# A fused attention and two-MLP kernel: weight conversion in two places of a slot, earlier stores and splits, identity products in front, the last output block in halves

## The chip, the cores and the metric

The kernel runs on one core of a Trainium2 chip. The metric is the device time in microseconds (us) of one execution. A core has TensorE (PE, matrix products into PSUM), VectorE (DVE), ScalarE (ACT), GpSimd (POOL) and SyncE (SP); DMAs are issued by SP, ACT and POOL queues. Each engine carries out its own instructions in the order in which the program issues them, and waits for semaphores of the others.

## The reference, cut to what matters

```python
B, H, S, Ns, D = 8, 8, 512, 32, 64
a = softmax(scale * x @ state.T);   xread = a @ state      # 512 rows per batch and head
a2 = softmax(scale * state @ x.T);  sread = a2 @ x         # 32 "states' rows" per batch and head
t = concat([xread, sread])          # 8 batches x 544 rows, 512 wide
t = ((t @ w1) * (t @ w2)) @ w3 @ w_out                      # first MLP
h = t @ w_in                                               # second MLP, 2048 wide
out = (h * clip(h + 3, 0, 6) / 6) @ w_out2
```

All inputs and the output are float32.

## The kernel before, in words

Products in full precision are made from a high part (`fp32r`, rounded) and a low part (the rest): three products high x high, high x low, low x high (`mm3`). ACT makes the high part (`rnd`, L71), DVE the low part (`rest`, L79). The program has four stages.

**Front, 0 to about 115 us.** Weights of the first MLP come in as 64-bit words (layout of the host), and DVE and ACT convert them to float32 (`Pipe`, L142 to L155), unit by unit. w3 @ w_out is multiplied out once (`ps_w`, L419), and attention of batch 0 and 1 runs between the units.

**Blocks, about 115 to 480 us.** One block `b` is one batch of 512 rows; it has eight slots `m` (block 0 starts at slot 4). Below, (b,m) is slot m of block b. One slot is, in TensorE's order: 12 products for `ps_ab` (two banks); the first half of the `x2` products of a slot issued two slots earlier (6); in even slots the 32 small products `ps_p` of a later slot pair; in some slots attention products of the next batch (`ps_s` in slot 0, `ps_e` in slot 4, `ps_r` in slot 6); the second half of the `x2` products. DVE and ACT serve it: `asb` (ACT copy of one bank), `ab` (DVE product of both banks, L529), `abh`/`abl` (high and low part), `ph`/`pl` (the same of `ps_p`), and the steps of attention. PSUM banks of the tag `b` go round in a ring of four: in slot (b,1) `ps_ab` takes the banks of `ps_p` of slot (b,0), which `pl` (DVE) frees; in slot 4, `ps_e` takes those of `ps_ab`, which `ab` frees.

Beside it runs `stream2`, which converts the 16 units of the second MLP's weights and stores them to DRAM for later. It is a generator, cut into pieces by `yield n`, where n is a cost. `before()` in a slot, after `ab`, adds `ROOM[m]` to an allowance and takes pieces until it is used up. One unit is on DVE: `ts` and `hd` (L473, L475), `w` (L478), the sum into `w` (L489, or L491 and L493), `cm` (four quarter sums, L507 to L510), and two low parts `sl` (768 and 1024 columns); on ACT: `sh` (two high parts, called by `parts`), and `hd` (unpack of the next unit, L445); on SP: one load of 1 MB, and the stores of `sh` and `sl` (`out_of_parts`).

**States, 480 to about 540 us.** `s_block` runs the 256 states' rows through the first MLP. It needs their high and low part `xs_hl`, which are made at the top of the last block (L749, L750).

**Second MLP, to the end.** Pairs of blocks go through a seven-product scheme (Strassen's, Winograd's form) with the stored weights: `gates` (L936), then `output` (L1097), for four pairs. The last pair also carries the states' rows. At the very end DVE adds and transposes the last two result tiles (`both(21, q)`), and SP stores them by four DMAs.

Of the kernel before, what the change touches and what calls it, by code (L numbers as in the profile page):

```python
# [19 lines left out]
def attn_moe_kernel(tc, xt_d, xn_d, bd_d, wa, wb, wc, wi, wo, out):  # L20
# [56 lines left out]
    def rest(out_, in_, hi, eng):  # L77
        e = nc.gpsimd if eng == "P" else nc.vector
        e.tensor_tensor(out=out_, in0=in_, in1=hi.bitcast(F32), op=ALU.subtract)  # L79
# [39 lines left out]

    ORDER = "oaoaoaoawwppppwwpppp"  # L120

    ROOM = (10, 7, 6, 6, 2, 6, 11, 9)


    class Pipe:
# [45 lines left out]


    x_t, A_t, st_t = {}, {}, {}
    xs_r = None
    room = 0

    def load_x(b):
# [6 lines left out]
    def attention(b, fine=False):  # L184
# [49 lines left out]
        def sread_out(ps):  # L234
            if b == B - 1:
                nc.scalar.copy(out=xs_r[:, :, b * NS:], in_=ps[:, :4 * NS].rearrange("p (c n) -> p c n", c=4))
                return
            xs = att.tile([128, 4, NS], F32, tag="xs", name="xs")
            nc.scalar.copy(out=xs.rearrange("p c n -> p (c n)"), in_=ps[:, :4 * NS])
            nc.sync.dma_start(out=xsd[:, :, b * NS:(b + 1) * NS], in_=xs)  # L240
# [103 lines left out]

    with tc.manual_schedule():
        make_identity(nc, ident)


        main = open_pool("main", bufs=1, side=left, reuse_waits="tile")
# [81 lines left out]
        def stream2():  # L431

            units = [x for u in range(8) for x in ((wi, u), (wo, u))]
            raws, hds = {}, {}

            def load(i):
                if i < len(units):
                    raw = raws[i] = cvs.tile([128, 4160], U16, tag="raw", name="raw", bufs=2)[:, :4100]
                    nc.sync.dma_start(out=raw[:, 1:4097], in_=units[i][0][units[i][1]].bitcast(U16))

            def unpack(i):
                if i < len(units):
                    hd = hds[i] = cvs.tile([128, 1024], U16, tag="hd", name="hd", bufs=2)
                    top = raws[i].bitcast(BF16)[:, 4:].rearrange("p (n k) -> p n k", k=4)[:, :, 0]
                    nc.scalar.activation(out=hd.bitcast(BF16), in_=top, func=AF.Prelu, scale=2.0 ** -112,  # L445
                                         alpha=2.0 ** 32)

            load(0)
            load(1)
            yield 0  # L450
            unpack(0)
            yield 0
            v = nc.vector
            def parts(h, w, cm):
                rnd(h[:, :768], w[:, :768], "A")
                rnd(h[:, 768:], cm, "A")

            def out_of_parts(src, u, h, l):
                for hl, t in enumerate((h, l)):
                    to = swi[u][hl].rearrange("p s k f -> p s (k f)") if src is wi else swo[hl][:, :, u, :]  # L460
                    for at, of, n in ((0, 2, 5), (5, 0, 2)):
                        nc.sync.dma_start(out=to[:, at:at + n, :],
                                          in_=t.bitcast(F32)[:, 256 * of:256 * (of + n)].rearrange("p (s e) -> p s e", e=256))

            prev = None
            for i in range(len(units) + 1):
                more = i < len(units)
                if more:
                    src, u = units[i]
                    hd, raw = hds.pop(i), raws[i]  # L470
                    ts = cvs.tile([128, 1024], U16, tag="ts", name="ts")
                    w = cvs.tile([128, 1024], F32, tag="w", name="w", bufs=2)
                    v.tensor_scalar(out=ts, in0=hd, scalar1=3, scalar2=0xFF80, op0=ALU.logical_shift_left,  # L473
                                    op1=ALU.bitwise_and)
                    v.tensor_scalar(out=hd, in0=hd, scalar1=3, scalar2=None, op0=ALU.logical_shift_left)  # L475
                    yield 2
                    g = raw.bitcast(U32).rearrange("p (n k) -> p n k", k=2)[:, :1024, 1]
                    v.scalar_tensor_tensor(out=w, in0=g, scalar=2.0 ** -36, in1=ts.bitcast(BF16), op0=ALU.mult,  # L478
                                           op1=ALU.mult)
                    raws.pop(i)  # L480
                    load(i + 2)
                if prev:
                    h, l = (cvs.tile([128, 1792], F32R, tag=f"s{hl}", name=f"s{hl}") for hl in "hl")
                    parts(h, *prev[2:])
                yield 3
                if more:
                    hb = hd.bitcast(BF16)
                    if src is wi:
                        v.tensor_tensor(out=w, in0=w, in1=hb, op=ALU.add)  # L489
                    else:  # L490
                        v.scalar_tensor_tensor(out=w[:, :512], in0=w[:, :512], scalar=-1.0, in1=hb[:, :512],  # L491
                                               op0=ALU.mult, op1=ALU.subtract)
                        v.tensor_tensor(out=w[:, 512:], in0=w[:, 512:], in1=hb[:, 512:], op=ALU.add)  # L493
                    unpack(i + 1)
                    yield 3
                if prev:
                    rest(l[:, :768], prev[2][:, :768], h[:, :768], "V")
                    yield 2
                    rest(l[:, 768:], prev[3], h[:, 768:], "V")
                    out_of_parts(*prev[:2], h, l)  # L500
                    yield 3
                if not more:
                    return
                cm = cvs.tile([128, 1024], F32, tag="cm", name="cm")
                a12, a22, a11, a21 = (w[:, 256 * k:256 * k + 256] for k in range(4))
                s1, s2, s4, s3 = (cm[:, 256 * k:256 * k + 256] for k in range(4))
                v.tensor_tensor(out=s1, in0=a21, in1=a22, op=ALU.add if src is wi else ALU.subtract)  # L507
                v.tensor_tensor(out=s3, in0=a11, in1=a21, op=ALU.subtract)
                v.tensor_tensor(out=s2, in0=s1, in1=a11, op=ALU.subtract)
                v.tensor_tensor(out=s4, in0=a12, in1=s2, op=ALU.subtract if src is wi else ALU.add)  # L510
                prev = src, u, w, cm
                yield 4
# [225 lines left out]
        for b in range(B):  # L738
# [5 lines left out]
                close_pool("cvs")  # L744
                wsq = open_pool("wsq", bufs=1, side=right, reuse_waits="tile")
            if b == B - 1:
                t = att.tile([128, T, DM], F32R, tag="xn", name="xs_hl").rearrange("p (i a) f -> p i (a f)", i=2)
                xs_h, xs_l = (t[:, i].rearrange("p (k f) -> p k f", k=KD) for i in range(2))
                rnd(xs_h, xs_r, "A")  # L749
                rest(xs_l, xs_r, xs_h, "V")  # L750
                s_block()
                close_pool("wsq")
                close_pool("att")
                xb = open_pool("xb", bufs=1, side=right, reuse_waits="tile")
                first = combos(0)
            A = A_t.pop(b)
            for m in range(0 if b else 4, M1):
                if m == (6 if b else 7) and b + 2 < B:
                    load_x(b + 2)

                def before():
                    nonlocal room
                    step()
                    room += ROOM[m]
                    while room > 0:
                        room -= next(second, 99)

                vn = 4 * b + m // 2 + 1

                def mid_():  # L770
                    if vn < 4 * B and m % 2 == 0:
                        p_mm(vn)
                        p_split(vn)
                    step()
                slot(b, m, A, before, mid_)
                if b == 0:
                    step()
# [239 lines left out]
        def output(p, ring, side):  # L1017
# [34 lines left out]
            def both(k, q):  # L1052
                result(k, q)
                leave(k, q)
# [28 lines left out]
            for v in range(28):  # L1083
# [4 lines left out]
                name = ("d1", "d3", "d2", "d3", "d2", "d1", "d2")[i]  # L1088
                hl = two(ring[v % 3])

                def main():
                    for q in range(2):
                        for k in range(2):
                            n = 2 * u + k
                            wh, wl = (t[:, 128 * q:128 * q + 128] for t in w_at(base, 8 * i + n))
                            for z, (a, x) in enumerate(((wh, hl[0]), (wh, hl[1]), (wl, hl[0]))):
                                nc.tensor.matmul(d[name][q], a, x[:, k, :], start=i < 3 and n == 0 and z == 0,  # L1097
                                                 stop=n == NG - 1 and z == 2, skip_group_check=True)

                def more():  # L1100
# [11 lines left out]
                                                 stop=i > 1 and n == NG - 1 and z == 2, skip_group_check=True)  # L1112
                if i == 6:
                    more()
                    main()
                else:
                    main()
                    more()
# [13 lines left out]
                side(v)  # L1132
            if states:
                states_out()
                for q in range(2):
                    both(21, q)
            else:
                for q in range(2):
                    result(21, q)
# [114 lines left out]
```

## Time and profile before

| | |
|---|---|
| median of 3 runs | 1231.1 us (1230.68 to 1233.33) |
| the profiled execution, its own time | 1234.02 us |
| its span, first to last instruction | 1232.2 us |
| TensorE busy | 1191.2 us (97%) |
| VectorE busy | 862.7 us (70%) |
| ScalarE busy | 551.9 us (45%) |
| chain that ended last | PE 82%, DVE 10%, DMA 4%, ACT 2% |

Busy time of TensorE counts its instructions from start to modelled end; what matters is where it stands idle, and the clock that it was granted (PEclk; 1.00 is 2.4 GHz, 0.50 is 1.2 GHz). The profiled execution is 2.92 us longer than the median of the runs.

### The profile page before, as it was taken

What the parts mean: (1) busy time and instruction counts of PE and PEld (TensorE: products, weight loads), DVE (VectorE), ACT (ScalarE), POOL (GpSimd) and SP (SyncE); (2) the same over time, 40 slices, a digit from 0 to 9 for tenths busy, and PEclk for the clock granted to TensorE, in tenths of its full rate; (3) what the DMA queues carried; (4) which work ended last, traced back from release to release, by engine and by line L of the source; (5) the groups of instructions that cost most, each with busy time, mean ns of one, the idle gap of its engine ahead of it and who ended that gap; (6) DMA issues with size and microseconds to landing.
All of it is one profiled execution on the core that took longest, in us unless ns stands there. A gap on an engine that the chain in (4) does not pass through costs nothing.

```text
span 1232.2 us, 17120 instructions
## 1 busy us (share of the span) xinstructions
PE 1191.2 (97%) x6688; PEld 943.4 (77%) x6688; DVE 862.7 (70%) x1220; ACT 551.9 (45%) x809; POOL 44.7 (4%) x59
## 2 busy tenths in 40 slices
PE   5989899999999999999999999999999999999997
PEld 2446676767777777978888888888888888888886
DVE  6976878888888464264767867687666886558483
ACT  3434454655454354244445434454344543334341
POOL 0000000000000000000101001010010100001100
PEclk9989999999999999999999999999999999999999
DMA  9751666485864210134889878998788987445973
GB/s 355 271 203 69 241 222 224 143 313 180 278 199 181 76 50 12 58 111 155 249 258 257 286 230 257 273 253 267 234 266 280 249 263 237 152 148 156 249 226 69
DMA packets 118576, 252.64 MB, mean 205 GB/s; under 512 B 45152, under 2 KB 63072, under 8 KB 111840
## 3 DMA queue, kind: packets, MB, share of 16 engines
q1 hardware_dynamic: 110288, 222.72, 52.6%
q0 software_dynamic: 7632, 27.79, 11.3%
q8 instruction: 52, 0.85, 0.3%
q10 hardware_dynamic: 576, 1.05, 0.2%
q14 instruction: 28, 0.23, 0.1%
HBM read 182.39 MB, written 47.64 MB: 187 GB/s over the span
## 4 chain that ended last, share of the span: by engine, by line
PE 82%; DVE 10%; DMA 4%; ACT 2%; issue 1%; SPq 0%; ACTq 0%; DVEq 0%
PE ps_d L1097 25%; PE ps L936 24%; PE x L88 4%; PE ps_ab L88 4%; PE ps_ab L90 4%; PE x L89 4%; PE x L90 4%; PE ps_ab L89 4%; PE ps_w L419 2%; PE ps_hs L936 2%; PE ps_so L1110 2%; PE ps_p L365 2%; DMA swoh<-sh 1%; DVE sl L79 1%; DMA wal<-swil 1%
## 5 line engine op out<-in xcount | busy, mean ns | idle before, releaser
L936 PE MATMUL ps<-xc,wah 128*128 128x512 f32 x512 | 157.9, 389 | 0.0
L79 DVE TENSOR_TENSOR hlj<-g,hlj 128x1024 fp32r<-128x1024 f32 x84 | 102.4, 1219 | 36.3 <-ACT hlj L71 36.2
L866 ACT ACTIVATE rl<-c,half 128x512 f32<-128x512 f32 x96 | 69.5, 724 | 117.2 <-DVE c L836 67.8
L936 PE MATMUL ps<-xc,wbh 128*128 128x512 f32 x384 | 118.3, 389 | 0.0
L1097 PE MATMUL ps_d<-hlj,wah 128*128 128x512 f32 x384 | 118.2, 389 | 0.0
L88 PE MATMUL ps_ab<-Ah,ph 128*128 128x512 f32 x256 | 105.2, 411 | 10.8 <-DVE pl L79 10.0
L88 PE MATMUL x<-abh,w3ph 128*128 128x512 f32 (+1 forms) x288 | 112.3, 390 | 0.0
L71 ACT ACTIVATE hlj<-g 128x1024 fp32r<-128x1024 f32 x84 | 88.6, 1057 | 52.1 <-PE ps_d L1097 48.2
L936 PEld LDWEIGHTS ps<-xc,wah 128*128 128x128 f32 x512 | 95.7, 188 | 19.5
L89 PE MATMUL x<-abl,w3ph 128*128 128x512 f32 (+1 forms) x288 | 109.0, 378 | 0.0
L90 PE MATMUL x<-abh,w3pl 128*128 128x512 f32 (+1 forms) x288 | 108.9, 378 | 0.0
L90 PE MATMUL ps_ab<-Ah,pl 128*128 128x512 f32 x256 | 102.6, 401 | 1.7 <-DVE pl L79 1.7
L89 PE MATMUL ps_ab<-Al,ph 128*128 128x512 f32 x256 | 102.7, 401 | 0.5 <-DVE Al L79 0.5
L936 PE MATMUL ps<-xc,wal 128*128 128x512 f32 x256 | 99.7, 389 | 0.6 <-DMA wal<-swil 0.6
L1097 PE MATMUL ps_d<-hlj,wbh 128*128 128x512 f32 x288 | 88.7, 389 | 0.0
L529 DVE TENSOR_TENSOR ab<-ps_ab,asb 128x512 f32<-128x512 f32 x64 | 44.0, 688 | 56.7 <-PE ps_ab L90 46.1
L1097 PEld LDWEIGHTS ps_d<-hlj,wah 128*128 128x128 f32 x384 | 72.1, 188 | 14.9
L936 PEld LDWEIGHTS ps<-xc,wbh 128*128 128x128 f32 x384 | 72.0, 188 | 15.0
L71 ACT ACTIVATE abh<-ab 128x512 fp32r<-128x512 f32 (+1 forms) x72 | 43.5, 604 | 77.1 <-DVE ab L529 77.1
L904 POOL DMA_DIRECT2D g<-g x41 | 35.7, 871 | 1102.9 <-DVE c L836 593.9
L936 PE MATMUL ps<-xc,wbl 128*128 128x512 f32 x192 | 74.7, 389 | 0.0
L1097 PE MATMUL ps_d<-hlj,wal 128*128 128x512 f32 x192 | 74.7, 389 | 0.0
(167 smaller groups left out, 2351.5 us busy)
## 6 DMA issues: line engine op xcount, KB each, us to landing
g<-g POOLq DMA_DIRECT2D x41, 512.0 KB, 6.9
wah<-swih SPq DMA_DIRECT2D x32, 512.0 KB, 4.5
wal<-swil SPq DMA_DIRECT2D x32, 512.0 KB, 5.3
wah<-swoh SPq DMA_DIRECT2D x32, 512.0 KB, 4.5
wal<-swol SPq DMA_DIRECT2D x32, 512.0 KB, 5.3
wbh<-swih SPq DMA_DIRECT2D x32, 384.0 KB, 5.1
wbl<-swil SPq DMA_DIRECT2D x32, 384.0 KB, 5.4
wbh<-swoh SPq DMA_DIRECT2D x32, 384.0 KB, 5.3
```

The lines of the kernel that those rows point to most:

```text
L71: nc.scalar.activation(out=out_, in_=in_, func=AF.Copy)
L79: e.tensor_tensor(out=out_, in0=in_, in1=hi.bitcast(F32), op=ALU.subtract)
L88: nc.tensor.matmul(ps, lh, rh, start=first, stop=False)
L89: nc.tensor.matmul(ps, lh, rl, start=False, stop=False)
L90: nc.tensor.matmul(ps, ll, rh, start=False, stop=last)
L365: nc.tensor.matmul(ps[c][32 * q:32 * q + 32, 256 * i:256 * i + 256], st_t[b][r, 2 * c + j, 32 * k:32 * k + 32], w12[mm // 2, 2 * c + j][r, ...
L419: nc.tensor.matmul(w3_ps[m], t[:, o:o + 128], wout[k], start=k == 0, stop=k == M1 - 1)
L529: nc.vector.tensor_tensor(out=ab[:, :n], in0=psb[:, :n], in1=a[:, :n], op=ALU.mult)
L866: nc.scalar.activation(out=rl, in_=c, func=AF.Relu, bias=half, scale=sign / 6.0)
L904: nc.gpsimd.dma_start(out=to, in_=of, accum_op=ALU.add)
L936: nc.tensor.matmul(ps, u[:, k, :], v[:, k, :], start=first and k == 0 and i == 0, stop=k == 1 and i == 2, skip_group_check=True)
L1097: nc.tensor.matmul(d[name][q], a, x[:, k, :], start=i < 3 and n == 0 and z == 0, stop=n == NG - 1 and z == 2, skip_group_check=True)
```

## The change

Five edits: the allowance of `stream2` is given out in two places of a slot (`pump(0)` after `ab`, as before, and `pump(1)` after `p_split` and attention's step), by a new table with other and, in sum, smaller numbers; the high parts of a unit are stored as soon as they are made; `xs_hl` is made right after the last `sread`, in slot (6,6), instead of at the top of block 7; 36 products of the identity with itself stand in front; and the last result tile is computed, added, transposed and stored in two halves of 256 columns, by the queues of SP and ACT.

```diff
-    ROOM = (10, 7, 6, 6, 2, 6, 11, 9)
+    ROOM = ((3, 3), (3, 4), (3, 3), (3, 3), (0, 1), (3, 3), (5, 5), (4, 6))
...
             if b == B - 1:
                 nc.scalar.copy(out=xs_r[:, :, b * NS:], in_=ps[:, :4 * NS].rearrange("p (c n) -> p c n", c=4))
+                t = att.tile([128, T, DM], F32R, tag="xn", name="xs_hl").rearrange("p (i a) f -> p i (a f)", i=2)
+                xs_hl.extend(t[:, i].rearrange("p (k f) -> p k f", k=KD) for i in range(2))
+                rnd(xs_hl[0], xs_r, "A")
+                rest(xs_hl[1], xs_r, xs_hl[0], "V")
                 return
...
         make_identity(nc, ident)
+        ps = bank("ps_i")
+        for i in range(36):
+            nc.tensor.matmul(ps[:, :128], ident, ident, start=True, stop=True)
...
                     parts(h, *prev[2:])
+                    out_of_part(*prev[:2], 0, h)
...
                     rest(l[:, 768:], prev[3], h[:, 768:], "V")
-                    out_of_parts(*prev[:2], h, l)
+                    out_of_part(*prev[:2], 1, l)
...
-                rnd(xs_h, xs_r, "A")
-                rest(xs_l, xs_r, xs_h, "V")
+                xs_h, xs_l = xs_hl
                 s_block()
...
+                def pump(i):
                     nonlocal room
-                    step()
-                    room += ROOM[m]
+                    room += ROOM[m][i]
                     while room > 0:
                         room -= next(second, 99)
+
+                def before():
+                    step()
+                    pump(0)
...
                     step()
+                    pump(1)
                 slot(b, m, A, before, mid_)
...
-                    main()
+                    main(states and u == 3)
...
-                for q in range(2):
-                    both(21, q)
+                both(21, 0)
+                t, to = small("c", 3), stg[21]
+                for f in range(2):
+                    cols, blocks = slice(256 * f, 256 * f + 256), slice(8 * f, 8 * f + 8)
+                    add(t[:, cols], d["d2"][1][:, cols], d["m1"][1][:, cols])
+                    nc.vector.transpose(out=to[:, blocks, 1, :], in_=t[:, cols])
+                    for g in range(4):
+                        (nc.scalar if g % 2 else nc.sync).dma_start(
+                            out=out[2 * p * ROWS + 256 * f:2 * p * ROWS + 256 * f + 256, 128 * g + 64:128 * g + 128]
+                            .rearrange("(b t) e -> t b e", t=32),
+                            in_=to[32 * g:32 * g + 32, blocks].rearrange("p b q e -> p b (q e)"))
```

How the edits move instructions. On VectorE, slot (1,0) before, from `ab` of the slot to `pl`; the five rows between `ab` and `abl` belong to units 2 and 1 of `stream2`:

```order
L529 TENSOR_TENSOR ab<-ps_ab_1042,asb 128x512
L473 TENSOR_SCALAR ts<-hd 128x1024
L475 TENSOR_SCALAR hd<-hd 128x1024
L478 SCALAR_TENSOR_TENSOR w<-raw,ts 128x1024
L489 TENSOR_TENSOR w<-w,hd 128x1024
L79 TENSOR_TENSOR sl<-w,sh 128x768
L79 TENSOR_TENSOR abl<-ab,abh 128x512
L79 TENSOR_TENSOR pl<-ps_p,ph 128x512 x2
```

The same stretch of VectorE after the change, and what follows up to the piece that `pump(1)` gives out:

```order
L536 TENSOR_TENSOR ab<-ps_ab_1079,asb 128x512
L479 TENSOR_SCALAR ts<-hd 128x1024
L481 TENSOR_SCALAR hd<-hd 128x1024
L79 TENSOR_TENSOR abl<-ab,abh 128x512
L79 TENSOR_TENSOR pl<-ps_p,ph 128x512 x2
L204 TENSOR_REDUCE mr<-ps_s 128x1
L205 TENSOR_SCALAR mr<-mr 128x1
L206 STREAM_TRANSPOSE sN<-ps_s 128x512
L204 TENSOR_REDUCE mr<-ps_s 128x1
L205 TENSOR_SCALAR mr<-mr 128x1
L206 STREAM_TRANSPOSE sN<-ps_s 128x512
L484 SCALAR_TENSOR_TENSOR w<-raw,ts 128x1024
```

In front of `abl` and `pl` only `ts` and `hd` are left; `w` now stands behind attention's rows (`mr`, `sN`), and the sum into `w` and the low part `sl` have moved to slot (1,1).

On ScalarE, from the copy of the last `sread` in slot (6,6) to the first copy of `s_block`, before:

```order
L236 COPY xs_r<-ps_r 128x4x32
L71 ACTIVATE wsh<-big_553 128x1024
L527 COPY asb<-ps_ab_4238 128x512
L71 ACTIVATE abh<-ab 128x512
L71 ACTIVATE wsh<-big_598 128x1024
L71 ACTIVATE xs_hl<-xs_r 128x1024
L527 COPY asb<-ps_sb_4279 128x256
```

The same stretch of ScalarE after the change:

```order
L236 COPY xs_r<-ps_r 128x4x32
L71 ACTIVATE xs_hl<-xs_r 128x1024
L71 ACTIVATE wsh<-big_590 128x1024
L534 COPY asb<-ps_ab_4278 128x512
L71 ACTIVATE abh<-ab 128x512
L71 ACTIVATE wsh<-big_635 128x1024
L534 COPY asb<-ps_sb_4316 128x256
```

The high part of `xs_hl` has moved from the end of the stretch to just behind `xs_r`; its low part moves the same way on VectorE.

On VectorE, the end of the program before:

```order
L1059 STREAM_TRANSPOSE so<-ps_so 128x2x8x32 x2
L836 TENSOR_TENSOR c<-ps_d_9915,m_9789 128x512
L1006 STREAM_TRANSPOSE stg<-c 128x16x32
L836 TENSOR_TENSOR c<-ps_d_9916,m_9790 128x512
L1006 STREAM_TRANSPOSE stg<-c 128x16x32
```

The end of VectorE after the change:

```order
L1067 STREAM_TRANSPOSE so<-ps_so 128x2x8x32 x2
L844 TENSOR_TENSOR c<-ps_d_9952,m_9826 128x512
L1014 STREAM_TRANSPOSE stg<-c 128x16x32
L844 TENSOR_TENSOR c<-ps_d_9953,m_9827 128x256
L1149 STREAM_TRANSPOSE stg<-c 128x8x32
L844 TENSOR_TENSOR c<-ps_d_9953,m_9827 128x256
L1149 STREAM_TRANSPOSE stg<-c 128x8x32
```

The second sum and transpose have become two of half the width each. Of the stores behind them, SP had four of 32x16x64; now SP and ACT have four each of 32x8x64.

## Rows read from the trace of the kernel before

**Rows 1.** The page, part 1: TensorE's busy time, share of the span, instructions.
```profile
PE 1191.2 (97%) x6688; PEld 943.4 (77%) x6688; DVE 862.7 (70%) x1220; ACT 551.9 (45%) x809; POOL 44.7 (4%) x59
```

**Rows 2.** What TensorE waited for between 100 and 360 us: total, times, longest.
```profile
PE ps_ab L88 <- DVE pl L79: 10.0, 6, 3.9
...
PE ps_e L215 <- DVE ab L529: 1.6, 2, 1.3
...
PE ps_ab L89 <- DVE Al L79: 0.5, 1, 0.5
```

**Rows 3.** By stretch: us, busy PE, PEld, DVE, ACT, POOL (count), PEclk, DMA share, GB/s.
```profile
120.00:480.00 360.00, 346.08 (x2572) 262.79 (x2565) 279.94 (x438) 185.23 (x303) 0.00 (x0) 0.99 0.53 180
...
152.00:157.00 5.00, 4.70 (x14) 3.71 (x15) 3.57 (x8) 2.03 (x5) 0.00 (x0) 0.66 0.84 316
...
177.80:402.26 224.46, 217.91 (x1597) 165.05 (x1598) 185.65 (x297) 118.56 (x194) 0.00 (x0) 0.98 0.63 214
...
402.26:455.50 53.24, 53.24 (x402) 40.95 (x402) 28.75 (x43) 23.74 (x41) 0.00 (x0) 1.00 0.23 73
...
480.00:484.00 4.00, 4.00 (x24) 4.00 (x22) 0.00 (x0) 0.37 (x1) 0.00 (x0) 0.57 0.01 4
...
1229.00:1230.00 1.00, 0.00 (x0) 0.00 (x0) 0.00 (x0) 0.00 (x0) 0.00 (x0) 0.50 1.02 215
```

**Rows 4.** Timeline: start, us, engine, work, [idle before <- releaser]; TensorE in (1,1), (1,4), (4,4).
```profile
152.30 0.50 PE L88 MATMUL ps_ab<-Ah,ph 128*128 128x512 f32 x1 [3.95 <-DVE pl L79]
...
177.80 0.66 PE L215 MATMUL ps_e<-ident,e 128*128 128x128 f32 x4 [0.32 <-DVE ab L529]
...
348.95 0.66 PE L215 MATMUL ps_e<-ident,e 128*128 128x128 f32 x4 [1.27 <-DVE ab L529]
```

**Rows 5.** Timeline of VectorE, slots (1,0) and (1,2).
```profile
145.74 1.22 DVE L478 SCALAR_TENSOR_TENSOR w<-raw,ts 128x1024 f32<-128x1024 uint32 x1
...
150.09 0.96 DVE L79 TENSOR_TENSOR sl<-w,sh 128x768 fp32r<-128x768 f32 x1 [1.88 <-ACT hd L445]
...
151.57 1.28 DVE L79 TENSOR_TENSOR pl<-ps_p,ph 128x512 fp32r<-128x512 f32 x2
...
167.99 0.69 DVE L79 TENSOR_TENSOR abl<-ab,abh 128x512 fp32r<-128x512 f32 x1 [1.74 <-ACT abh L71]
```

**Rows 6.** Timeline of ScalarE, slot (1,0).
```profile
147.24 0.85 ACT L71 ACTIVATE sh<-w 128x768 fp32r<-128x768 f32 x1 [5.44 <-DMA swih<-sh]
```

**Rows 7.** Timeline where the states' rows are split, 471 to 480 us.
```profile
471.76 1.23 DVE L79 TENSOR_TENSOR wsl<-big,wsh 128x1024 fp32r<-128x1024 f32 x1 [1.28 <-ACT wsh L71]
...
477.10 1.04 ACT L71 ACTIVATE xs_hl<-xs_r 128x1024 fp32r<-128x1024 f32 x1
...
478.19 0.39 PE L88 MATMUL ps_sb<-xs_hl,wsh 128*128 128x256 f32 x1 [0.69 <-ACT xs_hl L71]
...
478.37 1.22 DVE L79 TENSOR_TENSOR xs_hl<-xs_r,xs_hl 128x1024 fp32r<-128x1024 f32 x1
...
479.64 0.38 PE L89 MATMUL ps_sb<-xs_hl,wsh 128*128 128x256 f32 x1 [1.07 <-DVE xs_hl L79]
```

**Rows 8.** Timeline of the start: TensorE's first weight loads, and one wait of VectorE.
```profile
13.50 2.07 PE L419 MATMUL ps_w<-wo,t 128*128 128x512 f32 x2 [13.50 <-DVE t L155]
...
14.52 0.33 PEld L419 LDWEIGHTS ps_w<-wo,t 128*128 128x128 f32 x1 [0.52 <-issue]
...
20.05 0.19 PEld L419 LDWEIGHTS ps_w<-wo,t 128*128 128x128 f32 x1 [0.24 <-issue]
...
28.14 0.69 DVE L204 TENSOR_REDUCE mr<-ps_s 128x1 f32<-128x512 f32 x1 [0.58 <-PE ps_s L200]
```

**Rows 9.** Timeline of the end; ahead of it a sum of 256 columns in `s_block`.
```profile
484.27 0.42 DVE L529 TENSOR_TENSOR ab<-ps_sb,asb 128x256 f32<-128x256 f32 x1 [4.68 <-PE ps_sb L90]
...
1226.18 0.71 DVE L1006 STREAM_TRANSPOSE stg<-c 128x512 f32<-128x512 f32 x1
...
1226.92 1.97 SPq L1013 DMA_DIRECT2D out_dram<-stg  x4
```

More of the change, by code (lines that the diff above doesn't have):

```diff
@@ L173, in attn_moe_kernel @@
     x_t, A_t, st_t = {}, {}, {}
-    xs_r = None
+    xs_r, xs_hl = None, []
     room = 0
@@ L456, in parts, with out_of_part @@
                 rnd(h[:, 768:], cm, "A")
[L458 to L463, printed above, removed]
+            def out_of_part(src, u, hl, t):
+                to = swi[u][hl].rearrange("p s k f -> p s (k f)") if src is wi else swo[hl][:, :, u, :]
+                for at, of, n in ((0, 2, 5), (5, 0, 2)):
+                    nc.sync.dma_start(out=to[:, at:at + n, :],
+                                      in_=t.bitcast(F32)[:, 256 * of:256 * (of + n)].rearrange("p (s e) -> p s e", e=256))
             prev = None
@@ L746, in attn_moe_kernel @@
             if b == B - 1:
-                t = att.tile([128, T, DM], F32R, tag="xn", name="xs_hl").rearrange("p (i a) f -> p i (a f)", i=2)
-                xs_h, xs_l = (t[:, i].rearrange("p (k f) -> p k f", k=KD) for i in range(2))
-                rnd(xs_h, xs_r, "A")
-                rest(xs_l, xs_r, xs_h, "V")
+                xs_h, xs_l = xs_hl
                 s_block()
@@ L759, in attn_moe_kernel @@
                     load_x(b + 2)
-                def before():
+                def pump(i):
                     nonlocal room
-                    step()
-                    room += ROOM[m]
+                    room += ROOM[m][i]
                     while room > 0:
                         room -= next(second, 99)
+                def before():
+                    step()
+                    pump(0)
                 vn = 4 * b + m // 2 + 1
@@ L1089, in output, with main @@
                 hl = two(ring[v % 3])
-                def main():
-                    for q in range(2):
+                def main(end=False):
+                    for q, f in ((0, slice(0, 512)), (1, slice(0, 256)), (1, slice(256, 512))) if end else (
+                            (q, slice(0, 512)) for q in range(2)):
                         for k in range(2):
@@ L1096, in main @@
                             for z, (a, x) in enumerate(((wh, hl[0]), (wh, hl[1]), (wl, hl[0]))):
-                                nc.tensor.matmul(d[name][q], a, x[:, k, :], start=i < 3 and n == 0 and z == 0,
+                                nc.tensor.matmul(d[name][q][:, f], a, x[:, k, f], start=i < 3 and n == 0 and z == 0,
                                                  stop=n == NG - 1 and z == 2, skip_group_check=True)
@@ L1134, in output @@
                 states_out()
-                for q in range(2):
-                    both(21, q)
+                both(21, 0)
[9 more added lines that the diff above has]
+                            in_=to[32 * g:32 * g + 32, blocks].rearrange("p b q e -> p b (q e)"))
             else:
```

## The prediction

> **What bounds the kernel now.** I read the page first: TensorE is busy 97% of the span [rows 1], so only its idle time, its slow clock, and the ends of the program can be won. Then the table of waits says what it waits for, and the table by stretch says where. Between 120 and 480 us it is busy 346.1 of 360 us [rows 3]: 13.9 us idle, and nearly all of it is a wait for VectorE (10.0 + 1.6 + 0.5 us [rows 2]), or the split of the states' rows (0.69 + 1.07 us [rows 7]). The stages behind 540 us the change leaves alone, but for the last tile.
>
> A wait costs more than itself. After the 3.95 us wait ahead of 152.30 [rows 4] the granted clock averages 0.66 over the next 5 us [rows 3]: 0.34 x 5 = 1.7 us of full-speed work lost. After the states' split it averages 0.57 over 4 us [rows 3]: another 1.7 us. The short wait of 1.27 us at 348.95 [rows 4] will count for itself alone.
>
> How much the blocks lose altogether is read without adding waits. From the transposes of slot (5,4) to those of (6,4), a block passes in 53.24 us, with TensorE never idle and the clock at 1.00; the four blocks from (1,4) to (5,4) take 224.46 us [rows 3], which is 224.46 - 4 x 53.24 = 11.5 us more. That is waits and slow clock together, with VectorE busy 185.65 of 224.46 us, 83% [rows 3].
>
> **Conversion in two places of a slot.** Take slot (1,0). TensorE stood 3.95 us because `pl`, which frees the banks for the next `ps_ab`, ran only at 151.57 [rows 4, 5]. Ahead of `pl` stood, of `stream2`: `ts` and `hd`, `w` (1.22 us), the sum into `w` (1024 columns like it, so 1.22 too), a hole of 1.88 us in which VectorE waited for ScalarE's unpack, and a low part of 0.96 us [rows 5]. The hole goes back to ScalarE, which stood 5.44 us until the store of the previous `sh` had landed [rows 6], with the unpack behind it. After the change only `ts` and `hd` stand there: 1.22 + 1.22 + 1.88 + 0.96 = 5.3 us less ahead of `pl`, more than the wait of 3.95 us. So this wait should go, and the slow clock behind it.
>
> But VectorE is the slower engine up to slot (1,4), so the gain there is counted along it. Up to the `ab` of (1,4), which TensorE waits for at 177.80 [rows 4], the new table leaves out the two low parts of unit 2 (0.96 + 1.22 = 2.2 us) and both holes that come from ScalarE's `sh` (1.88 and 1.74 us [rows 5]): 5.8 us. Against it, the `sh` pair of unit 1 now stands on ScalarE between attention's exponentials and the `asb` of slot (1,1). Its time is 0.85 us for 768 columns [rows 6] and, by columns, some 1.1 us for 1024, 2.0 us together, of which VectorE fills 1.2 us with the moved `w`: a new hole of 0.8 us. That leaves 5.0 us. TensorE's own loss up to there was 0.5 + 3.95 + 0.3 + 1.7 = 6.4 us [rows 2 to 4], so some 1.4 us of wait stays at `ps_e` of (1,4). I take 5.0; the bounds are 0 and 6.4.
>
> In blocks 1 to 5, behind (1,4), the same shape comes back: at most 2.4 us of `stream2` now stands ahead of `pl` in slot 0 (`ts`, `hd`, `w`). What stays is `ps_e` in slot 4, where the pieces of slot 3 stand ahead of `ab` as before; the rows for such a wait are 0.32 and 1.27 us [rows 4]. I take 0.5 us for each of four blocks, nearer to the first because slot 2 is lighter now: 11.5 - 2.0 = 9.5 us; bounds 0 and 11.5.
>
> The sum of the table falls from 57 to 52 a block, so the last units move from slot (5,1) to (5,6). Block (5,4) to (6,4) had VectorE busy only 28.75 of 53.24 us [rows 3]: that is the cover. If it failed, block 5 would pay like the others, 11.5 / 4 = 2.9 us.
>
> **High parts stored at once.** I cost this at nothing by itself. SP has no other reason to hold these stores back than a load of the next batch that was written ahead of them; the stores' landing still has 5.44 us waits as its bound [rows 6], and two slots or more between most pairs of `sh` are what hides it now. Behind the waiting store on SP stand the next loads of x, which are needed several slots later.
>
> **States' rows.** The high part moves to slot (6,6), where VectorE has a hole of 1.28 us ahead of 471.76, and nothing waits until 477 us [rows 7]; its own low part takes 1.22 us [rows 7]. So 0.69 + 1.07 us of wait go, with the 1.7 us of slow clock: 3.5 us; bounds 1.8 (the clock falls anyway) and 3.5.
>
> **Identity products.** TensorE is idle until 13.50; its first products then start 0.85 us apart (0.33 + 0.52) and from 19.6 us on 0.43 us apart [rows 8]. 36 products of 128 columns are 72 passes of a quarter of that: 7.7 us at the fast pace, 15.4 at the slow one, and with 6.1 us of slow pace first some 11, so they fit ahead of 13.50. Seven passes at double pace cost 3.0 us. But VectorE sets the pace of the front, and it waited only 0.58 us for TensorE, ahead of 28.14 [rows 8]. I take 0.6 us; bounds 0 and 3.0.
>
> **Last tile in halves.** Two halves of a sum (0.42 us for 256 columns) replace one, and each transpose of 0.71 us becomes two of half that [rows 9]; the last of them ends as before, near 1226.9. The gain is in the stores: four issues took 1.97 us on SP, 0.49 each, so the last began at 1228.40 [rows 9]. With half of the data issued 0.7 us earlier, and ACT's queue beside SP's, the last begins at 1226.92 + 0.49 = 1227.41 or, if SP is still busy with the first half, 1227.7: 0.7 to 1.0 us earlier. I take 0.9; bounds 0 and 1.5, the 1.97 us of issues less a single one. The DMA engines are full at 1.02 between 1229 and 1230 [rows 3], so the data itself does not go faster. The Trainium skill, "DMA: Bandwidth & Descriptors", section "Issuing engines are not separate DMA queues", says the same from its side: all queues run on the same 16 engines, and a second one saves only issue time. By that rule the most would be 1.0 us, and without it, with two queues moving data beside each other, the 1.5 us of the bound; the full engines speak for the rule.
>
> **The sum.** 5.0 + 9.5 + 3.5 + 0.6 + 0.9 = 19.5 us off the profiled execution's own time of 1234.0, so 1214.5. That execution stands 2.9 us above the median of the runs, 1231.1; the same gain off the median gives **1211.6 us**.
>
> **The rivals.**
> - *VectorE's lag only moves.* With the pieces behind `pl`, `ab` of the next slot comes late instead, and `ps_e` or `ps_ab` wait there long enough for the clock to fall: like 152.30, but of the 2.4 us kind, 2.4 + 1.7 = 4.1 us. For it: VectorE was busy 83% of these blocks, with the rest bunched. Against: 53.24 us at full clock would need only 4 x 53.24 = 213 us for its 185.65 us, 87%. In three blocks it would cost 12.3 us more: 1224.
> - *The last units spoil block 5.* It pays 2.9 us, as above: 1214.5.
> - *Better still.* All of 6.4 + 11.5 + 3.5 goes, and the start gives 3.0: with 0.9 at the end 25.3 us, 1205.8.
> - *Slower: stores ahead of loads on SP.* A store of `sh` waits on SP for ScalarE, and x of the next batch stands behind it. x is asked for in slot 6 and needed in slot 0 of the next block, two slots or 13 us of the 53.24 later; from a hold above that, attention and with it a block stalls. A hold of 20 us in five blocks would cost 5 x (7 + 1.7) = 43 us: 1255. Against it: ScalarE's longest wait for a store was 5.4 us [rows 6].
>
> **How the numbers follow.** My forecast 0.60 (its own range 1208 to 1217), lag that moves 0.18, block 5 0.10, better still 0.08, slower 0.04. The range 1206 to 1221 takes in the forecast, block 5, most of "better still" and the milder half of the moved lag, some 0.8. About 0.2% (2.5 us) is what a measurement of this kernel can tell from no change. All cases but the last are faster by more; a lag that moves in all blocks could leave nothing, so faster 0.94, same 0.02, slower 0.04.
>
> **What the new profile would show.** Right: waits of TensorE for `pl` gone in slot 0, no clock below 1.00 between 120 and 480 us, blocks of 53 to 54 us, up to 1.4 us left at `ps_e` of (1,4); no wait and no slow clock at `s_block`; passes 0.43 us apart from the first real product on; last issue near 1227.5. Wrong: new waits for `ab` in slots 3 and 4 above 2 us with slow clock behind; ScalarE still waiting 4 us and more for stores; identity products running beyond 13.5 us; or the front's time back at 120 us as before.

## Result: 12.0 us less, where 19.5 were forecast

The changed kernel takes 1219.51 us (median of 4 runs, 1218.92 to 1220.74) beside 1231.54 of the kernel before (4 runs, 1230.68 to 1233.33): ratio 0.9902, 95% interval 0.9885 to 0.9919. A second measurement gave 0.9898 (0.9885 to 0.9911). The forecast of 1211.6 was 7.9 us too low; the time lies in its range, near the upper end. The profiled execution took 1218.92 us, with a span of 1217.1 beside 1232.2.

The page, part 1, and what TensorE waited for between 100 and 480 us, answer to [rows 1] and [rows 2]:

```profile
PE 1192.5 (98%) x6766; PEld 949.0 (78%) x6766; DVE 861.4 (71%) x1222; ACT 553.0 (45%) x809; POOL 44.7 (4%) x59
```

```profile
PE ps_s L200 <- DMA xr<-in_xt_dram: 5.6, 1, 5.6
PE ps_ab L88 <- DVE pl L79: 1.1, 2, 0.9
```

The 12 us of waits for VectorE are gone but for 1.1. In their place stands one wait of 5.6 us, not there before and not for VectorE: the scores of batch 2 wait for `xr`, their x. The view by stretch says what it costs beside itself; it answers to [rows 3]:

```profile
120.00:480.00 360.00, 353.33 (x2647) 271.54 (x2646) 281.50 (x444) 192.17 (x313) 0.00 (x0) 0.99 0.55 183
143.00:149.00 6.00, 0.75 (x32) 0.20 (x16) 3.95 (x9) 1.60 (x3) 0.00 (x0) 0.79 1.01 414
149.00:154.00 5.00, 4.67 (x12) 1.79 (x13) 2.39 (x6) 0.78 (x2) 0.00 (x0) 0.57 0.79 325
177.36:391.93 214.57, 214.36 (x1608) 163.35 (x1600) 181.31 (x292) 117.48 (x192) 0.00 (x0) 1.00 0.67 221
391.93:445.17 53.24, 53.24 (x409) 40.95 (x401) 33.83 (x51) 25.68 (x44) 0.00 (x0) 1.00 0.37 125
```

Four blocks pass in 214.57 us at full clock, beside 224.46 before; the loss sits in one place, 143 to 154 us, where TensorE stands still, the granted clock falls to a mean of 0.57, and the DMA engines are full (1.01, 414 GB/s).

Where in the program the time went is read from the same products in both kernels: the first row of `ps_e` transposes in block 0, those of slots (1,4) and (6,4), and the first product of the stage behind the blocks. The timeline of the kernel before, with what SP issued ahead of the scores of batch 2:

```profile
118.56 0.60 PE L215 MATMUL ps_e<-ident,e 128*128 128x128 f32 x4
...
135.40 0.34 SPq L439 DMA_DIRECT2D raw<-in_wo_dram  x1
...
136.27 0.42 SPq L181 DMA_DIRECT2D xr<-in_xt_dram  x1
136.78 1.15 SPq L462 DMA_DIRECT2D swih<-sh  x2
...
144.84 1.94 PE L200 MATMUL ps_s<-xr,br 128*64 128x512 f32 x8
...
176.82 0.66 PE L215 MATMUL ps_e<-ident,e 128*128 128x128 f32 x4
...
455.43 1.09 PE L215 MATMUL ps_e<-ident,e 128*128 128x128 f32 x8
...
568.47 0.62 PE L936 MATMUL ps<-xc,wah 128*128 128x512 f32 x2
```

The timeline of the changed kernel, from its first products to its last stores:

```profile
1.36 10.76 PE L353 MATMUL ps_i<-ident 128*128 128x128 f32 x72 [1.36 <-POOL ident masks.py:199]
13.49 10.57 PE L426 MATMUL ps_w<-wo,t 128*128 128x512 f32 x24 [1.37 <-DVE t L155]
...
118.20 0.60 PE L215 MATMUL ps_e<-ident,e 128*128 128x128 f32 x4
...
137.85 0.34 SPq L446 DMA_DIRECT2D raw<-in_wo_dram  x1
138.29 0.84 SPq L468 DMA_DIRECT2D swih<-sh  x2
139.23 0.87 SPq L180 DMA_DIRECT2D br<-in_bd_dram  x1
140.15 0.56 SPq L181 DMA_DIRECT2D xr<-in_xt_dram  x1
...
149.33 3.68 PE L200 MATMUL ps_s<-xr,br 128*64 128x512 f32 x8 [5.58 <-DMA xr<-in_xt_dram]
...
177.36 0.87 PE L215 MATMUL ps_e<-ident,e 128*128 128x128 f32 x6
...
445.17 1.09 PE L215 MATMUL ps_e<-ident,e 128*128 128x128 f32 x8
...
460.54 1.06 ACT L71 ACTIVATE xs_hl<-xs_r 128x1024 fp32r<-128x1024 f32 x1
...
461.63 1.23 DVE L79 TENSOR_TENSOR xs_hl<-xs_r,xs_hl 128x1024 fp32r<-128x1024 f32 x1 [1.42 <-ACT xs_hl L71]
...
467.08 0.28 PE L88 MATMUL ps_sb<-xs_hl,wsh 128*128 128x256 f32 x1
...
554.40 0.62 PE L944 MATMUL ps<-xc,wah 128*128 128x512 f32 x2
...
1209.74 0.69 DVE L844 TENSOR_TENSOR c<-ps_d,m 128x512 f32<-128x512 f32 x1 [0.67 <-PE ps_d L1106]
...
1212.10 2.55 SPq L1151 DMA_DIRECT2D out_dram<-stg  x4
1212.11 1.93 ACTq L1151 DMA_DIRECT2D out_dram<-stg  x4
```

From issue to landing `xr` took 8.4 us in the kernel before and 9.0 in the changed one, by the view of that tile. So before the change x was there at 136.27 + 8.4 = 144.7 and was needed at 144.84: it came in time with some 0.1 us to spare, and no view of waits shows that. After the change it was asked for 3.9 us later, behind a weight load that waited for VectorE until 137.85 (before: 135.40) and behind the store of a high part; TensorE was there 1.1 us earlier (149.33 - 5.58 = 143.75). These differences are the wait: 2.45 us from the later weight load, 1.43 from the longer way from its issue to that of `xr` (2.30 us beside 0.87), 0.6 from the longer transfer and 1.1 from TensorE, 5.6 in all.

Differences of those rows give the gain by stage (us). For the forecast I split its sum at the same places: 5.0 plus the 1.4 of wait that it left at (1,4) stand ahead of the transposes of that slot, and 9.5 less 1.4 behind. "x early" is the first experiment below.

| stage | before | after | gain | forecast | x early | its gain |
|---|---|---|---|---|---|---|
| start to `ps_e` of block 0 | 118.56 | 118.20 | 0.4 | 0.6 | 118.41 | 0.2 |
| to `ps_e` of (1,4) | 58.26 | 59.16 | **-0.9** | **6.4** | 51.87 | 6.4 |
| to `ps_e` of (6,4) | 278.61 | 267.81 | 10.8 | 8.1 | 269.03 | 9.6 |
| to the first product behind the blocks | 113.04 | 109.23 | 3.8 | 3.5 | 109.24 | 3.8 |
| to the last tile's first sum | 655.63 | 655.34 | 0.3 | 0 | 654.98 | 0.6 |
| to the end | 8.10 | 7.36 | 0.7 | 0.9 | 7.37 | 0.7 |
| span | 1232.2 | 1217.1 | 15.1 | 19.5 | 1210.9 | 21.3 |

One row is off. (The last sum starts at 1224.10 us in the kernel before, at 1209.74 in the changed one and at 1203.53 with x early.)

### The profile page after: what moved, and what is told of

It is laid out like the page before. It is cut to its first block, busy times and chain, and to the rows that moved or that the text cites. A ratio compares the mean times of both kernels' runs of the same rounds, so it can differ in the third digit from the quotient of the medians.

```text
span 1217.1 us, 17294 instructions
## 1 busy us (share of the span) xinstructions
PE 1192.5 (98%) x6766; PEld 949.0 (78%) x6766; DVE 861.4 (71%) x1222; ACT 553.0 (45%) x809; POOL 44.7 (4%) x59
## 4 chain that ended last, share of the span: by engine, by line
PE 89%; DVE 6%; DMA 3%; ACT 1%; issue 0%; SPq 0%; ACTq 0%; DVEq 0%
PE ps_d L1106 25%; PE ps L944 24%; PE x L88 5%; PE x L89 5%; PE x L90 5%; PE ps_ab L88 5%; PE ps_ab L90 5%; PE ps_ab L89 5%; PE ps_p L372 2%; PE ps_hs L944 2%; PE ps_so L1119 2%; PE ps_w L426 1%; PE ps_s L200 1%; PE ps_r L230 1%; DMA wal<-swil 1%; DMA swih<-sh 1%
```

## Experiments

Theory: the forecast missed because x of batch 2 is late, held on SP by what now stands ahead of it. Rivals: the wait only covers another for VectorE; or the two places are worth less than forecast. Ratios are to the kernel before on the same chip, with their 95% intervals.

**x early.** One move in the changed kernel:

```diff
-                if m == (6 if b else 7) and b + 2 < B:
+                if m == 6 and b + 2 < B:
                     load_x(b + 2)
```

> The changed kernel with one move: the load of batch 2's x stands ahead of slot 6 of block 0, as in all other blocks, and no longer ahead of slot 7. On SP it then stands ahead of the weight load that waited for VectorE until 137.85 us and ahead of the store of a high part at 138.29. Theory (x is late): the forecast missed because this one load is held on SP by the two and then shares full DMA engines with the store; x is there by about 137 us, the wait of 5.6 us ahead of the scores of batch 2 goes and with it the slow clock behind it, some 1.8 us: 7.4 us less, 1219.5 to about 1212. Rival (VectorE's lag only moves): with x there TensorE runs into the wait for VectorE that the 5.6 us now cover, at ps_e of slot (1,4) or ps_ab of slots (1,0) to (1,2), of 3 us and more with slow clock: 1216 to 1219.5. Rival (full engines): the weight load behind x comes late in its place and the unpack on ScalarE waits for it: 1215 to 1220.

Measured: 1213.41 us beside 1233.83, ratio 0.9824 (0.9805 to 0.9843). SP issues `xr` at 129.88, it lands in 6.7 us; that row, and the waits of TensorE between 100 and 480 us:

```profile
129.88 0.50 SPq L181 DMA_DIRECT2D xr<-in_xt_dram  x1
...
PE ps_e L215 <- DVE ab L536: 1.0, 1, 1.0
PE ps_ab L88 <- DVE pl L79: 0.9, 1, 0.9
```

By stretch, the hole is closed though the DMA engines are as full as before:

```profile
143.00:149.00 6.00, 6.00 (x54) 3.51 (x48) 5.90 (x13) 1.85 (x4) 0.00 (x0) 1.00 1.01 405
149.00:154.00 5.00, 5.00 (x24) 4.14 (x23) 3.01 (x6) 4.41 (x9) 0.00 (x0) 1.00 0.64 208
```

Its timeline in slot (1,4) shows what TensorE meets next:

```profile
170.28 0.66 PE L215 MATMUL ps_e<-ident,e 128*128 128x128 f32 x4
...
171.92 0.66 PE L215 MATMUL ps_e<-ident,e 128*128 128x128 f32 x4 [0.98 <-DVE ab L536]
```

The theory holds. The rival of a covered wait is right in kind (0.98 us for VectorE that the late x had hidden) and wrong in size. Between 143 and 154 us no wait for a DMA is left in the table of waits: the full DMA engines now carry loads and stores that nobody waits for there.

Because the gain is the point, both kernels were run again on one chip:

> The changed kernel once more, beside the next one on the same chip: 0.990 of the kernel before, with a wait of 5 us and more for x of batch 2.

> The changed kernel with x of batch 2 loaded ahead of slot 6 of block 0 once more, beside the changed kernel on the same chip. Theory: 7.4 us less than the changed kernel, between 5 and 9; 0.983 of the kernel before. Rival (the difference of the two runs so far comes from the chips): 3 us or less.

1219.28 and 1213.20 us, ratios 0.9898 (0.9885 to 0.9911) and 0.9849 (0.9836 to 0.9862): the move is worth 6.1 us, a little under the 7.4 expected. The wait for x was 6.6 us in the first and absent in the second.

**High parts stored late again.** The changed kernel without the early store:

```diff
                     parts(h, *prev[2:])
-                    out_of_part(*prev[:2], 0, h)
...
                     rest(l[:, 768:], prev[3], h[:, 768:], "V")
+                    out_of_part(*prev[:2], 0, h)
                     out_of_part(*prev[:2], 1, l)
```

> The changed kernel with one part undone: high parts are stored together with the low parts, as before the change. Theory (x is late, by the store in front of it): x of batch 2 is issued some 0.9 us earlier and without 0.9 MB in front of it, which at the 414 GB/s of that stretch is 2.2 us: it lands some 3 us earlier, and 2.5 us of the wait of 5.6 us stay, which come from the weight load in front. If late stores cost ScalarE nothing else, 1216. Rival (the early stores are worth something by themselves): ScalarE waits 2 us and more for the landing of the previous store in each high part again and VectorE behind it; then 1220 or more in spite of the earlier x.

1216.35 us, ratio 0.9851 (0.9828 to 0.9875): faster than the changed kernel, by 3 us of the medians and 6 of the ratios. The trace is plainer: the wait for x shrinks but does not go,

```profile
145.70 2.52 PE L200 MATMUL ps_s<-xr,br 128*64 128x512 f32 x8 [3.44 <-DMA xr<-in_xt_dram]
```

so 2.1 of the 5.6 us go with the store ahead of x, and 3.4 stay: they come from the weight load ahead of both, which the new table delays, and from TensorE's earlier arrival. (The front of this execution ended 1.5 us earlier, with `ps_e` of block 0 at 116.71, so its times are compared from there.) Counted from `ps_e` of block 0, the weight load goes out after 19.6 to 19.7 us in every run with the new table and after 16.8 to 16.9 in every run with the old one. In the five executions where both load and store stand ahead of x the wait is 5.6 to 7.3 us, so the part of the store is 2.1 to 3.8. Two issues of 640 and 256 KB are 0.92 MB, 2.2 us at the 414 GB/s of that stretch. The Trainium skill, "DMA: Bandwidth & Descriptors", section "Queues, rings and completion order", says that each DMA engine takes the descriptors of a queue in the order of its ring; the 2.1 us agree with that, and the longer waits were not taken apart.

**Both moves together.** x early, and high parts stored late:

```diff
-                if m == (6 if b else 7) and b + 2 < B:
+                if m == 6 and b + 2 < B:
...
-                    out_of_part(*prev[:2], 0, h)
...
+                    out_of_part(*prev[:2], 0, h)
                     out_of_part(*prev[:2], 1, l)
```

> Both moves together: x of batch 2 loaded ahead of slot 6 of block 0, and high parts stored with the low parts. Theory (the early stores are worth nothing once x is out of their way, as the prediction costed them): within 2.5 us of the kernel with x early alone, 1212. Rival (they free ScalarE's buffer in time, and are worth the holes of 1.9 and 1.7 us that VectorE had before): 1215 or more, with waits of ScalarE for sh above 4 us.

1212.55 us, ratio 0.9819 (0.9799 to 0.9838), the same as with x early alone. ScalarE waits 3.1 us in all for stores of `sh` between 100 and 480 us, 3.6 in the changed kernel, 17.0 in the kernel before: the new table takes these waits away with or without the early stores. The rival falls.

**The early stores alone.** The kernel before, with this part of the change and nothing else:

```diff
                     parts(h, *prev[2:])
+                    out_of_part(*prev[:2], 0, h)
...
-                    out_of_parts(*prev[:2], h, l)
+                    out_of_part(*prev[:2], 1, l)
```

> The kernel before with one part of the change alone: high parts are stored at once; table, states' rows, both ends and the load of x as before. In the kernel before, x of batch 2 landed at 144.7 us and was needed at 144.8, with the store of a high part right behind it on SP. Theory (the early store is worth nothing by itself here and costs where x has no time to spare): ScalarE's waits for the landing of the store shrink, but pl stays late by the pieces in front of it, and x lands later by what now stands ahead of it: 1231.5 within 2.5 us, with a wait of the scores of batch 2 of some 2 us. Rival (the hole of 1.88 us ahead of pl came from the late store): 3 us and more faster, 1228.5 or less.

1233.20 us beside 1232.91, ratio 1.0011 (0.9998 to 1.0023): nothing in all. In its trace ScalarE's waits for stores of `sh` shrink from 17.0 to 7.1 us, `pl` still costs TensorE 8.3 us, and x comes late here too. SP issued it at 137.77, it took 9.1 us, and that is when TensorE goes on:

```profile
137.77 0.62 SPq L181 DMA_DIRECT2D xr<-in_xt_dram  x1
...
147.00 1.94 PE L200 MATMUL ps_s<-xr,br 128*64 128x512 f32 x8 [2.03 <-ACT hd L445]
```

The row names ScalarE, but 137.77 + 9.1 = 146.9 is when x landed, the last of the things waited for. With the old table these 2 us cost nothing in the end: the `pl` wait of slot (1,0) is 0.88 us in place of 3.95 [rows 4]. By the stages of the table, 55.65 us pass up to `ps_e` of (1,4), 2.6 less than before, and 281.66 from there to (6,4), 3.1 more: the early stores win something in the first stretch and lose it behind, in larger waits for `pl` and `ab` there (6.6 and 3.2 us beside 5.2 and 1.6). Why those grow was not tried.

**The old table.** The other edits kept, first with x as in the changed kernel, then with x early:

```diff
-    ROOM = ((3, 3), (3, 4), (3, 3), (3, 3), (0, 1), (3, 3), (5, 5), (4, 6))
+    ROOM = ((10, 0), (7, 0), (6, 0), (6, 0), (2, 0), (6, 0), (11, 0), (9, 0))
```

> The changed kernel with the old table: all conversion pieces of a slot ahead of it (10, 7, 6, 6, 2, 6, 11, 9, second place 0), all other edits kept. Theory (the two places carry the gain of blocks 1 to 5): the waits for pl in slot 0 come back, some 10 us: 1228 to 1232. Rival (the early stores carry it, since they take away the wait of 5.4 us of ScalarE and with it the hole of 1.9 us ahead of pl): waits for pl of at most 1.5 us, 1219 to 1223.

> The old table (all pieces ahead of the slot) with x of batch 2 loaded ahead of slot 6 of block 0, all other edits kept. Against the same kernel with the new table (1213.4 beside 1233.8 for the kernel before), this is the whole worth of the two places. Forecast's terms: 5.0 + 9.5 = 14.5 us, about 1228. Rival (the old table with early stores loses much less, since its holes came from ScalarE's wait for the store): 1222 or less.

1227.52 us, ratio 0.9944 (0.9923 to 0.9966), and 1227.35, ratio 0.9957 (0.9939 to 0.9976). Waits of TensorE in the second:

```profile
PE ps_ab L88 <- DVE pl L79: 7.8, 6, 2.7
PE ps_e L215 <- DVE ab L536: 3.2, 2, 2.0
PE ps_ab L89 <- DVE Al L79: 0.5, 1, 0.5
```

The waits for VectorE are back. With x early in both, the table is worth 0.9957 - 0.9824 = 1.3% or 16 us (about 3 either way, from the two intervals), by the two profiled executions 1225.24 - 1212.71 = 12.5; beside the second run of x early, on the same chip, 0.9957 - 0.9849 = 1.1% or 13 us; forecast 14.5. By stage it is 2.8 us up to (1,4) (54.67 us here) and 10.7 from there to (6,4) (279.70). In the first stretch the two edits overlap: with x in time, the early stores with the old table bring it from 58.26 to 54.67 us, the new table with late stores to 51.89 (both moves together, above), and the two to 51.87. With the old table an early x is worth nothing that the ratios show: VectorE's wait stands behind it.

**x late in every block.** The changed kernel, with slot 7 for all blocks:

```diff
-                if m == (6 if b else 7) and b + 2 < B:
+                if m == 7 and b + 2 < B:
```

> The changed kernel with the load of x ahead of slot 7 in every block, as block 0 has it, and not ahead of slot 6. Theory (what counts is the time between asking for x and slot 0, one slot of some 6.6 us, against 6 to 9 us from issue to landing behind the stores of the conversion): the scores of batches 3, 4 and 5 wait too, 2 to 5.6 us each with the slow clock behind it: 3 x (2 to 7.4) us more, 1225 to 1241. Rival (the late x was special to block 0, whose weight load waited for VectorE until 137.85 us): no new waits above 1 us, 1219 to 1221.

1226.84 us, ratio 0.9951 (0.9933 to 0.9969), some 6 us over the changed kernel by the ratios. The scores of batches 3 to 5 wait, less from block to block:

```profile
206.80 3.56 PE L200 MATMUL ps_s<-xr,br 128*64 128x512 f32 x8 [2.80 <-DMA xr<-in_xt_dram]
...
263.91 2.65 PE L200 MATMUL ps_s<-xr,br 128*64 128x512 f32 x8 [2.17 <-ACT ph L71]
...
320.12 1.94 PE L200 MATMUL ps_s<-xr,br 128*64 128x512 f32 x8 [1.31 <-ACT ph L71]
```

In the last two ScalarE is named, but x was issued at 253.59 and 309.87 and took 10.2 us each, so it landed at 263.8 and 320.1. The three waits add to 6.3 us, the lower end of what was expected. From the issue of x to TensorE's arrival there were 6.6, 8.2 and 8.9 us, for transfers of 9.3, 10.2 and 10.2. Block 0 waits longest, 5.6 us, because its x goes out last: at 139.69, 3.6 us ahead of TensorE, behind the late weight load.

**States' rows late.** The split put back in front of the product with W:

```diff
...
-                rnd(xs_hl[0], xs_r, "A")
-                rest(xs_hl[1], xs_r, xs_hl[0], "V")
                 return
...
-                xs_h, xs_l = xs_hl
...
+                rnd(xs_h, xs_r, "A")
+                rest(xs_l, xs_r, xs_h, "V")
```

> The changed kernel with one part undone: the split of the states' rows stands in front of the product with W, behind slot (6,7), as before. Forecast's term: 0.69 + 1.07 us of wait and 1.7 us of slow clock come back there, 3.5 us in all, 1219.5 to 1223; in the profile two waits at ps_sb and a granted clock near 0.57 over the 4 us behind them. Rival (the clock falls only behind longer waits, and the early split takes VectorE's time in front): 1.8 us or less, 1219.5 to 1221.3, with the clock at 1.00.

1221.93 us, ratio 0.9918 (0.9889 to 0.9947): too near the changed kernel to tell, and its wait for x was 7.3 us in the profiled execution. The trace of the place itself tells more:

```profile
468.75 0.38 PE L88 MATMUL ps_sb<-xs_hl,wsh 128*128 128x256 f32 x1 [0.69 <-ACT xs_hl L71]
...
470.20 0.38 PE L89 MATMUL ps_sb<-xs_hl,wsh 128*128 128x256 f32 x1 [1.07 <-DVE xs_hl L79]
```

```profile
470.00:475.00 5.00, 4.80 (x32) 4.47 (x33) 0.99 (x3) 1.60 (x3) 0.00 (x0) 1.00 0.00 0
```

The same two waits as in [rows 7], to the hundredth, but a clock of 1.00 behind them, where it was 0.57 before [rows 3]. From `ps_e` of (6,4) to the first product behind the blocks it takes 111.52 us, 2.3 more than the changed kernel; the kernel before took 3.8 more. The early stores alone leave the split late too: the same two waits, a clock of 0.57 again from 480 to 484 us, and 113.01 us for the stage. So the waits, 1.8 us, are the sure part of the term; the slow clock followed them in two executions of three, and whether the kernel or the execution decides that is not shown.

**Both ends as before.** Without the identity products, and the last tile whole:

```diff
-        ps = bank("ps_i")
-        for i in range(36):
-            nc.tensor.matmul(ps[:, :128], ident, ident, start=True, stop=True)
...
-                    main(states and u == 3)
+                    main()
...
-                both(21, 0)
...
+                for q in range(2):
+                    both(21, q)
```

> The changed kernel with both ends as before: without the 36 identity products, and with the last tile in one piece. Forecast's terms: 0.6 us at the front, 0.9 at the end, 1.5 together, about 1221 (too little for the rounds to tell from nothing; the profile tells them apart). In the profile: the first sum of VectorE that waits for TensorE at 28.1 us and not 27.0, the front back to 0.6 us or less of loss at 120 us; 8.1 us from the last sum's start to the end and not 7.4. Rival (the early products give the whole of the passes at double pace): 3.0 us at 120 us, 1223.5.

1220.45 us, ratio 0.9908 (0.9880 to 0.9935), no difference that the intervals can tell. In the trace `ps_e` of block 0 stands at 118.60, 0.40 us later than in the changed kernel, and from the last tile's first sum to the end it takes 1217.4 - 1209.34 = 8.06 us beside 7.36. The halves give 0.7 us in every execution: 7.33 to 7.43 us with them, 8.06 to 8.10 without. The identity products are less sure: `ps_e` of block 0 stands at 118.56 to 118.66 in the three executions without them and at 116.71 to 118.85 in the ten with them (118.20 and 117.51 in the changed kernel itself). By the medians, 118.60 and 117.90, they give 0.7 us, less than the 2.1 us by which that row scatters.

## Why the forecast was right in sign and 7.5 us too generous

**The step that failed** is what the prediction made of SP's queue, in two of its terms. "High parts stored at once" was costed at nothing because "behind the waiting store on SP stand the next loads of x, which are needed several slots later". For batch 2 that is false. Block 0 asks for x in slot 7, not 6, so there is one slot of time and not two, and the time was already used up: 0.1 us to spare before the change. And "Conversion in two places" was counted on VectorE, ScalarE and TensorE alone: it also moves `w`, for which the weight load ahead of x waits on SP, so that this load goes out 2.8 us later in its block. Of the 5.6 us of wait the late weight load, with TensorE's earlier arrival, is the larger part (3.4 us stay without the store), the store the smaller (2.1). With the old table the store alone makes a wait of 2.0 us; with neither there was none.

The rival "stores ahead of loads on SP" had the order on the queue right and said "x is asked for in slot 6"; it got 0.04 because its slack of 13 us was that of the later blocks. Its hold was another: the store did not wait for ScalarE, it went out right behind the weight load (138.29), and that load was held by VectorE. The stall came in one block: 5.6 us of wait and, since the scores then took 3.68 us in place of 1.94, another 1.7 of slow clock, 7.3 us in all. That is the whole difference between -0.9 and 6.4 in the table, and x early brings it back.

**Conversion in two places.** Right, and well sized where x is in time: 6.4 us up to the transposes of (1,4) as forecast, then a wait of 0.98 us at `ps_e` where 1.4 were foretold, and 9.6 us over the next blocks beside 8.1. The waits for `pl` are gone but for 0.9 us, with the slow clock behind them, and come back with the old table. The rival that VectorE's lag only moves did not come: no wait for `ab` above 0.98 us. The last units did not spoil block 5: 53.24 us as in [rows 3], with VectorE busy 33.83 of it.

**States' rows:** 3.8 us beside 3.5, of which the run that undoes it shows 2.3, at full clock. **Identity products:** 0.4 us in the profiled pair and 0.7 by the medians of all executions, beside 0.6; as that row scatters by more, the agreement is partly luck. **Last tile:** 0.7 beside 0.9.

**From profile to median.** The profiled executions differ by 15.1 us, the medians by 12.0. The forecast took its whole gain off a median that lay 2.9 us under the profiled execution; but that execution was slower than all the runs beside it, and the profiled one of the changed kernel the fastest of its own four. So of the 7.5 us missing, 4.4 are missing in the trace (7.3 lost to x, 2.9 more than forecast elsewhere), and 3.1 in this step. In the second measurement the medians lay 13.6 us apart. Which waits vary from run to run in the kernel before was not tried.

## What to carry to other kernels

When a store or a load moves forward on a queue, or one that stands there comes to wait longer for an engine, read for every load behind it when it lands and when it is first needed, in each block and not only in the steady ones: a load that lands 0.1 us in time shows in no table of waits and pays for the whole shift. Here, asking for one load a slot earlier, which cost nothing that the runs show, was worth 6.1 us, about half of what the whole change had brought. Take a kernel's gain from medians, and a wait's price without the slow clock as the sure part of it.

## What the runs showed of the hardware

The transfer of 1 MB of x for batch 2 took 6.5 to 7.6 us in the four runs that asked for it early, 8.3 and 8.4 where it went out 0.9 us behind a weight load of 1 MB, and 9.0 to 10.8 behind that load and a store of 0.9 MB, with the DMA engines' share near 1.0. The weight load at 128.40 us of the kernel before, also 1 MB, took 5.1. The same pair of waits, 0.69 and 1.07 us, was followed by a granted clock of 0.50 (1.2 GHz) between 481 and 483 us in the kernel before and with the early stores alone, and by 1.00 (2.4 GHz) with the states' rows late. Behind the 5.6 us wait for x the mean was 0.57 over 5 us, behind the wait of 0.98 us in the run with x early 1.00.
